# Packed attention and gated feed-forward in one kernel: another order of the first batch's small steps

## The chip, the cores and the metric

The kernel runs on one core of one Trainium2 chip. A core has TensorE (PE, matrix products; its weight loads are listed as PEld), VectorE (DVE), ScalarE (ACT), GpSimd (POOL) and SyncE (SP), which here issues nearly all DMAs. Each engine takes its own instructions in the order written, and waits on semaphores for the others. The metric is the device time of one launch in microseconds (us), the median of the runs shown.

## The reference

Eight batches, eight heads, 576 positions, head size 64. Every head packs its sequence into 32 rows and attends to these; the result goes through a gated feed-forward of width 1536.

```python
scale = 1.0 / np.sqrt(q.shape[-1])
def sm_attn(qq, kk, vv):
    s = scale * np.matmul(qq, kk.transpose(0, 1, 3, 2))
    s = s - np.max(s, axis=-1, keepdims=True)
    a = np.exp(s)
    a = a / (np.sum(a, axis=-1, keepdims=True) + 1e-09)
    return np.matmul(a, vv)
p_packed = sm_attn(p, k, v)                  # (8, 8, 32, 64)
out = sm_attn(q, p_packed, p_packed)         # (8, 8, 576, 64)
x = out.transpose(0, 2, 1, 3).reshape(4608, 512)
return ((x @ w_a) * (x @ w_b) @ w_out).astype(np.float32)
```

q, k, v and p arrive as float32. The three weight matrices arrive in 64 bits a number, and the kernel makes float32 of them itself.

## The kernel before

**Attention.** `stage1(b, e)` (L270 on) computes p_packed of batch `b` for one half `e` of the heads: scores on PE (L276), maximum on DVE (L282), exponential on ACT (L294), sums and reciprocal on DVE (L298, L301), transposes of the exponentials on PE (L315, L316), their copies to `a1T` by ACT (L317, L318), the product with v on PE (L325), and the scaling on DVE (L331). `turned` transposes p_packed (L262) and copies it to `ppT` (L264). `stage2(b, e)` is the second attention (L340 to L371). Both are Python generators: each `yield` ends a step, and the plan says when the next one is emitted.

**v.** The product at L325 reads tile `vt`, which `load_v` fills with four DMAs (two at L171 of 256 KB, two at L175 of 32 KB). From batch 1 on both halves share one buffer: half 1 of batch 1 can be loaded once the L325 of half 0 has read it.

**Weights.** They come in 36 pieces of 512 KB: four for each of the six chunks of two feature tiles (w_a and w_b), twelve for w_out. Step `A` (L203, ACT) and step `B` (L211 on ACT, or L208 on DVE or POOL, as the digit of `WAYS` for that piece says) prepare the two words, step `C` (L214, DVE) joins them to float32 in `w_ab` or `wo_f32`, and `D` (L239 on ACT, L91 on POOL) splits a piece of w_out into high and low parts. There are twelve piece buffers; each `C` frees one and asks for the next pieces (L224, L231).

**Feed-forward.** For batch 0, `g_tiles` (L395) multiplies ppT with a chunk of `w_ab`; `mm1` (L416) takes 24 products a feature tile, ACT and DVE make h from them (L428, L431, L435, L91), and `mm2_part` (L442) multiplies h with w_out: for each feature tile four token tiles with three products each, 12 products of 512 columns. All sums of one batch's feed-forward stand in PSUM until the last feature tile. The later batches use other forms of the same products (L766, L807).

**Order.** Nothing is scheduled by the framework: what Python emits is each engine's order. `START` is the list of steps before the first feature tile of batch 0. After that, `between()` is called twice for each feature tile in `mm1` (24 slots) and once for each of nine feature tiles in the second product, and emits the steps that `PLAN_0` has for this slot: `A` to `D`, the loads (`Lk`, `Lq`, `Lv`, `Lp`), `r0` and `r1` (next step of `stage1` of batch 1, half 0 or 1), `s0` and `s1` (the same for `stage2`), `k` and `q` (turns of k and q), `P0` (`turned`). Where a step stands in the list is where its instructions stand on every engine that it uses, DMA issues included. SP issues DMAs in that order; a buffer that isn't free holds up SP and all that stands behind.

Of the kernel before, what the change touches and what calls it, by code (L numbers as in the profile page):

```python
# [19 lines left out]
def tile_packed_attn_gated_ffn(  # L20
# [21 lines left out]
    B, H, S, D = q.shape  # L42
# [13 lines left out]
    NB = 2  # L56
# [36 lines left out]
    def bank():  # L93
        return ps_x.tile([P, 512], F32, name="x")

    def bank_pair(s=False):
        return ps_s.tile([P, 2, 512], F32, name="s") if s else ps_m.tile([P, 2, 512], F32, name="m")

    def work(b, name, shape, tag=None):
        if b == 0:  # L100
            return scratch.tile(shape, F32, name=name)
        return wk.tile(shape, F32, name=tag, bufs=2 if tag == "t1" else 1)
# [91 lines left out]
    def xT_cols(b, key, u, h, cols=slice(0, HS)):  # L194
        return xTs[b, key][h // R][64 * u:64 * u + 64, h % R, cols]
# [9 lines left out]
    def low_word(raw, way):  # L205
        low = raw[..., 0]
        if way:
            (nc.vector if way == 1 else nc.gpsimd).tensor_scalar(  # L208
                out=low, in0=low, scalar1=2.0 ** -29, scalar2=7.0, op0=ALU.mult, op1=ALU.min)
        else:  # L210
            nc.scalar.activation(out=low, in_=low, func=AF.Copy, scale=0.93 * 2.0 ** -29)  # L211
# [56 lines left out]
    def stage1(b, e):  # L268


        s = bank_pair(b or e == 0)
        first = b < 2
        parts = [(0, 0, 0, HS)] + ([(1, TR, 0, 2 * P), (1, 0, 2 * P, TR)] if first else [(1, 0, 0, HS)])
        for u, c, t, n in parts:
            for r in range(R):
                nc.tensor.matmul(  # L276
                    out=s[J * r:J * r + J, u, c:c + n], lhsT=pT[64 * u:64 * u + 64, 2 * r + e, :],
                    rhs=xT_cols(b, "k", u, 2 * r + e, slice(t, t + n)), start=True, stop=True)
        s = s[:, :, 0:HS]
        yield  # L280
        nmx = sm.tile([P, 1], F32, name="nmx")
        nc.vector.tensor_reduce(out=nmx, in_=s, axis=AXY, op=ALU.max)  # L282
        nc.vector.tensor_scalar(out=nmx, in0=nmx, scalar1=-scale, scalar2=None, op0=ALU.mult)
        if b > NB:
            yield
        a1 = work(b, f"a1_{e}", [P, S], "t1")
        rs = sm.tile([P, 1], F32, name="rs")
        if first:
            exps = [(a1, s, rs)]
        else:  # L290
            rs2 = sm.tile([P, 1], F32, name="rs2")
            exps = [(a1[:, 2 * TR:S], s[:, :, 0:2 * P], rs), (a1[:, 0:2 * TR], s[:, :, 2 * P:HS], rs2)]
        for dst, src, acc in exps:
            nc.scalar.activation(  # L294
                out=dst.rearrange("p (u t) -> p u t", u=2), in_=src, func=AF.Exp, bias=nmx, scale=scale, accum_out=acc)
        yield
        if first:
            nc.vector.tensor_scalar(out=rs, in0=rs, scalar1=1e-9, scalar2=None, op0=ALU.add)  # L298
        else:
            nc.vector.tensor_scalar(out=rs, in0=rs, scalar1=rs2, scalar2=1e-9, op0=ALU.add, op1=ALU.add)  # L300
        nc.vector.reciprocal(out=rs, in_=rs)  # L301
        yield
        a1T = work(b, f"a1T_{e}", [P, NT, P], "t2")
        rest = 2 * P if first else 0
        chunks = [P * i + ((HS + TR) * u if first else 2 * TR + 2 * P * u) for i in range(2) for u in range(2)]
        if b or e:
            pair = bank_pair(b)
            tp, tq = pair[:, 0, :], pair[:, 1, :]
        else:
            tp, tq = bank(), bank()  # L310
        if b == 0:
            chunks = [(HS + TR) * u + i for i in range(2) for u in range(2)]
        step = 1 if b else 2
        for i, c in enumerate(chunks):
            nc.tensor.transpose(tp[:, P * i:P * i + P], a1[:, c:c + step * (P - 1) + 1:step], ident)  # L315
        nc.tensor.transpose(tq[0:64, 0:P], a1[:, rest:rest + 2 * TR], ident)  # L316
        nc.scalar.copy(out=a1T[:, 0:4, :].rearrange("p i t -> p (i t)"), in_=tp)  # L317
        nc.scalar.copy(out=a1T[0:64, 4, :], in_=tq[0:64, 0:P])  # L318
        yield
        pps = bank_pair(True)[:, 0, :] if b else bank()  # L320
        vt = vts.pop((b, e))
        for i in range(NT):
            n = P if i < 4 else 64
            for r in range(R):
                nc.tensor.matmul(  # L325
                    out=pps[J * r:J * r + J, 0:D], lhsT=a1T[0:n, i, J * r:J * r + J],
                    rhs=vt[0:n, r, i, :], start=(i == 0), stop=(i == NT - 1))
        if e == 0:
            pp[b] = sm.tile([P, E + 1, D], F32, name="pp", bufs=1)
        for i in range(e, E + 1, E):  # L330
            nc.vector.tensor_scalar(out=pp[b][:, i, :], in0=pps[:, 0:D], scalar1=rs, scalar2=None, op0=ALU.mult)  # L331
        yield
# [145 lines left out]
    def drain(g):  # L478
        for _ in g:
            pass  # L480

    def emit(b, plan, tasks={}):

        for name in plan.split():
            if name in tasks:
                next(tasks[name], None)
                continue
            if name == "Z":
                warm_first()
                continue  # L490
            if name in "Ww":
                warm(9 if name == "W" else 1)
                continue
            if name in "ABCD":
                convert(name)
                continue
            what, e = name[:-1], int(name[-1])
            n = b + (e // 2 if b or what[0] == "L" else 0)
            if n >= B:
                continue  # L500
            if what == "S":
                if e == 0:
                    st[b] = [stage1(b, 0), stage1(b, 1), stage2(b, 0), stage2(b, 1)]
                next(st[b][e])
            elif what == "s":
                next(st[b][2 + e], None)
            elif what == "r":
                next(st[b][e], None)
            elif what == "T":
                turn_p(n)  # L510
            elif what == "P":
                turned(ppT[:, b % 2:b % 2 + 2], pp.pop(b), b % 2)
            elif what in ("k", "q"):
                turn(what, n, e % 2) if b else turn_first(what, e)
            elif what == "Lk":
                load(k, "k", n, e % 2)
            elif what == "Lq":
                load(q, "q", n, e % 2)
            elif what == "Lv":
                load_v(n, e % 2)  # L520
            elif what == "Lp":
                load_p(n)
# [8 lines left out]
        nc.tensor.matmul(out=x[:, 0:2 * P], lhsT=zero[:, 0:P], rhs=zero, start=True, stop=True)  # L531

    FIRST = ("k0 P0 K1 k2 q0 q1 v0 q2 v1 w1 w1 w1 w1 w1 w1 w1 w1 w1 w1 w1")
    START = ("Z Z Z Z T0 k0 k1 k2 k4 k3 q0 S0 S1 r0 r1 q1 q2 r1 r0 r0 r1 q4 r0 r1 q3 P0 s0 s1 B W A s0 B A A B s0 A s0 C B s1 C s1 s0 B C s1 A s1 B C Lp2 A A B s0 g s1 s0 g w s1 g C B B B C A Lk2 A C A B C A A B B Lk3 C C")
    WAYS = ("000000021020002100012012011200010010")
    TURN = ("1101110010")
    SUBS = ("0000")

    PLAN = (" |  |  | S0 | r0 | r0 |  | r0 |  | r0 Lv1 ; S1 | r1 | r1 q0 Lk2 | r1 | r1 | q1 Lk3 Lv2 P0 |  ; s0 | s0 s0 | s0 T2 | "
            "s0 Lp4 | s0 s1 | s1 s1 | s1 | s1 | s1 | t0 t1 t2 t3 u0 | k2 |  | k3 Lq2")  # L540
    PLAN = dict(enumerate(PLAN.split("|")))
    PLAN_0 = ("A | C C | B A B A | B C C B C | A A | C | B Lv0 | C B A T0 k0 Lp2 | A A B C Lq0 | C k1 | A B A B A C | S0 B | B A r0 | C C C | B A | | C C B r0 r0 D A A | S1 C D | B C B B A D | r1 C | A A D | r0 Lv1 Lq1 T2 | | q0 B r1 C B D r1 C | | A D B | C A r1 A B D | Lk2 B C B q1 D Lk3 A A P0 | C s0 s0 D C Lp4 A B | s1 s0 | Lv2 | D | s0 s1 s0 | k2 s0 s1 C k3 | s1 | | Lq2 D s0 s1 s1 Lq3 s1")
    PLAN_0 = dict(enumerate(PLAN_0.split("|")))

    pieces = [(c, n) for c in range(NC) for n in range(4)] + [(NC, f) for f in range(NFT)]
# [12 lines left out]
    def convert(x):  # L558
# [14 lines left out]
        elif x == "B":  # L573
            low_word(raw, int(WAYS[pieces.index((c, n))]))
        else:
# [18 lines left out]
    def next_g(b):  # L594

        if b:
            g_tiles(b, (0, 1), (2,), s=True)
            yield
            return
        late = []  # L600
        g_tiles(b, (0, 1), late=late)
        yield
        for x in late:
            lo_part(*x)
            yield
# [15 lines left out]
    tasks = {"g": next_g(0)}  # L621
    emit(0, START, tasks)
    drain(tasks["g"])
# [55 lines left out]
    for b in range(NB):  # L679
        plan = dict(PLAN if b else PLAN_0)  # L680
        slot, tasks, late_steps = [0], {"g": next_g(b + 1)} if b == 0 else {}, [""]
# [260 lines left out]
    for n in range(LAST):  # L942
        b, ft = NB + n // NFT, n % NFT
# [55 lines left out]
```

## Time and profile before

| | |
|---|---|
| median of 3 runs | 705.21 us (704.41 to 705.64) |
| profiled execution, whole | 705.02 us |
| its span on the core | 703.2 us |
| PE busy | 695.9 us (99%) |
| DVE, ACT, POOL busy | 448.5, 363.7, 412.7 us |
| HBM | 85.92 MB read, 15.73 MB written |

All times below count from the start of the span; 1.8 us of the execution lie outside it. An engine's busy time is the time in which an instruction of it runs; what stands in brackets behind an idle time is what ended it. The first batch's first product (L416) runs from 27.65 to 78.1 us, its second (L442) from 78.54 on; the sixteen DMA engines are busy nearly all of the time until then.

### The profile page before, as it was taken

How to read it: one execution, taken by the hardware profiler on the slowest of the kernel's cores; microseconds unless marked ns; L12 is line 12 of the kernel's file. 1: busy time of each engine (PE TensorE's matmuls, PEld its weight loads, DVE VectorE, ACT ScalarE, POOL GpSimd, SP SyncE). 2: the span in 40 equal slices, each digit the busy share in tenths (PEclk: the TensorE clock that was granted, in tenths of full speed). 3: DMA queues.
4: the chain of work that ended last, by engine and by line, in shares of the span. 5: the costliest groups of instructions: out<-in, count | busy, mean ns of one | idle time of the engine just before them, and what ended most of it. 6: DMA issues, size and time to landing. Idle time of an engine off the chain costs nothing.

```text
span 703.2 us, 14176 instructions
## 1 busy us (share of the span) xinstructions
PE 695.9 (99%) x5542; PEld 573.2 (82%) x5542; DVE 448.5 (64%) x822; ACT 363.7 (52%) x731; POOL 412.7 (59%) x323
## 2 busy tenths in 40 slices
PE   8999999999999999999999999999999999999998
PEld 6488878888788878888888887888888878888886
DVE  3998664567266679566765778665785667754432
ACT  4988734544244556545554455554545446544520
POOL 0557652337155778646864588655776578856520
PEclk9999999999999999999999999999999999999999
DMA  9999955677164727356434653556245323133002
GB/s 309 381 229 312 273 108 105 238 185 202 56 167 142 178 83 169 111 147 177 105 95 124 174 161 95 140 171 158 69 131 143 106 91 120 61 122 118 1 1 75
DMA packets 180371, 102.57 MB, mean 146 GB/s; under 512 B 145744, under 2 KB 161744, under 8 KB 174928
## 3 DMA queue, kind: packets, MB, share of 16 engines
q1 hardware_dynamic: 179888, 101.08, 50.7%
q8 instruction: 43, 0.70, 0.4%
q10 hardware_dynamic: 416, 0.59, 0.2%
q14 instruction: 24, 0.20, 0.1%
HBM read 85.92 MB, written 15.73 MB: 145 GB/s over the span
## 4 chain that ended last, share of the span: by engine, by line
PE 94%; ACT 1%; DVE 1%; POOL 1%; DMA 1%; issue 1%; SPq 0%; DVEq 0%; POOLq 0%; ACTq 0%
PE x L766 38%; PE m L807 30%; PE m L416 7%; PE x L821 5%; PE m L442 5%; PE s L325 2%; PE s L340 1%; PE m L592 1%; PE s L276 1%; PE x L395 1%; DMA raw<-in_moe_w_b_dram 1%; PE s L315 1%; POOL h_lo L91 1%; PE m L531 1%; DVE w_ab L214 0%
## 5 line engine op out<-in xcount | busy, mean ns | idle before, releaser
L766 PE MATMUL x<-wo,h_hi 128*128 128x512 f32 (+1 forms) x776 | 249.1, 391 | 0.0
L91 POOL TENSOR_TENSOR h_lo<-asb,h_hi 128x576 fp32r<-128x576 f32 x96 | 140.2, 1460 | 88.0 <-ACT h_hi L435 44.3
L766 PEld LDWEIGHTS x<-wo,h_hi 128*128 128x128 f32 x776 | 140.7, 188 | 21.8 <-ACT gs L827 0.9
L766 PE MATMUL x<-wo,h_lo 128*128 128x512 f32 (+1 forms) x388 | 152.1, 392 | 0.0
L91 POOL TENSOR_TENSOR G_lo<-gs,G_hi 128x640 fp32r<-128x640 f32 x72 | 112.8, 1572 | 30.7 <-ACT G_hi L842 30.4
L766 PEld LDWEIGHTS x<-wo,h_lo 128*128 128x128 f32 x388 | 72.9, 188 | 11.8
L91 POOL TENSOR_TENSOR A_lo<-gs,A_hi 128x256 fp32r<-128x256 f32 x36 | 27.1, 754 | 87.1 <-ACT A_hi L830 87.1
L889 DVE TENSOR_TENSOR d<-m,d 128x576 f32<-128x576 f32 (+1 forms) x73 | 54.1, 741 | 35.2 <-ACT d L885 34.5
L902 DVE TENSOR_TENSOR asb<-m,d 128x288 f32<-128x288 f32 x72 | 32.5, 451 | 65.4 <-ACT c L898 62.0
L898 ACT COPY c<-m 128x288 f32<-128x288 f32 x72 | 28.7, 399 | 82.5 <-PE m L807 82.5
L776 DVE TENSOR_TENSOR part<-x,part 128x512 f32<-128x512 f32 (+1 forms) x65 | 44.1, 678 | 38.5 <-PE x L766 38.5
L807 PE MATMUL m<-tx_hi,G_hi 128*128 128x288 f32 x216 | 63.8, 295 | 0.0
L807 PE MATMUL m<-tx_hi,G_lo 128*128 128x288 f32 x216 | 63.7, 295 | 0.0
L827 ACT COPY gs<-x 128x512 f32<-128x512 f32 x36 | 21.1, 587 | 81.6 <-PE x L821 81.6
L807 PE MATMUL m<-tx_lo,G_hi 128*128 128x288 f32 x216 | 63.3, 293 | 0.0
L842 ACT CAST G_hi<-gs 128x640 fp32r<-128x640 f32 x72 | 52.2, 729 | 15.0 <-POOL gs L836 14.5
L885 ACT COPY d<-m 128x576 f32<-128x576 f32 (+1 forms) x73 | 46.7, 639 | 20.0 <-PE m L807 19.7
L852 ACT CAST h_hi<-asb 128x576 fp32r<-128x576 f32 x72 | 49.0, 680 | 11.5 <-DVE asb L916 11.5
L807 PEld LDWEIGHTS m<-a_hi,G_hi 128*128 128x128 f32 x144 | 27.0, 187 | 31.8 <-issue 17.4
L836 POOL TENSOR_TENSOR gs<-gs 128x512 f32<-128x512 f32 x36 | 46.6, 1294 | 2.1 <-DVE gs L833 1.7
L807 PE MATMUL m<-a_hi,G_hi 128*128 128x288 f32 x144 | 46.6, 324 | 0.0
L915 DVE TENSOR_TENSOR m<-m,c 128x288 f32<-128x288 f32 x72 | 33.4, 464 | 16.4 <-PE m L807 14.7
(169 smaller groups left out, 1550.0 us busy)
## 6 DMA issues: line engine op xcount, KB each, us to landing
wr<-w_kept SPq DMA_DIRECT2D x36, 1024.0 KB, 5.1
nat<-in_k_dram SPq DMA_DIRECT2D x56, 144.0 KB, 5.0
nat<-in_q_dram SPq DMA_DIRECT2D x56, 144.0 KB, 5.3
vt<-in_v_dram SPq DMA_DIRECT2D x28, 256.0 KB, 3.6
out_dram<-part SPq DMA_DIRECT2D x27, 256.0 KB, 2.0
raw<-in_moe_w_a_dram SPq DMA_DIRECT2D x12, 512.0 KB, 7.7
raw<-in_moe_w_b_dram SPq DMA_DIRECT2D x12, 512.0 KB, 8.5
raw<-in_moe_w_out_dram SPq DMA_DIRECT2D x12, 512.0 KB, 7.2
```

The costliest lines, as they stand in the source:

```text
L91: return eng.tensor_tensor(out=dst, in0=src, in1=hi.bitcast(F32), op=ALU.subtract)
L416: nc.tensor.matmul(out=ps[:, half, 0:HS], lhsT=gt[:, kt, ft % 4, cols], rhs=at[:, kt, HS * half:HS * half + HS], start=(n == 0 and kt == 0 ...
L442: nc.tensor.matmul(out=o[:, cols], lhsT=ht[:, c0:c0 + P], rhs=wt[:, cols], start=(ft == 0 and n == 0), stop=(ft == NFT - 1 and n == 2))
L766: nc.tensor.matmul(out=o[:, cols], lhsT=ht[:, c0:c0 + P], rhs=wt[:, cols], start=(ft == fts[0] and n == 0), stop=end)
L776: nc.vector.tensor_tensor(out=parts[i][:, cols], in0=o[:, cols], in1=parts[i][:, cols], op=ALU.add)
L807: nc.tensor.matmul(out=bank[:, n % 2, 0:HS], lhsT=g, rhs=t, start=(first and i == 0), stop=(i == 2), skip_group_check=True)
L821: nc.tensor.matmul(out=gps[e][J * r:J * r + J, :], lhsT=ppT[rows, 2 * (b % 2), r, :], rhs=w[rows, r, :], start=True, stop=True)
L836: nc.gpsimd.tensor_tensor(out=gs[:, 2:4].rearrange("p a u f -> p a (u f)"), in0=gs[:, 0:2].rearrange("p a u f -> p a (u f)"), in1=s2.unsqu ...
L842: nc.scalar.copy(out=G_hi[:, n % 3], in_=gs[:, 1:6, n % 2])
L852: nc.scalar.copy(out=view(h_hi[ft]), in_=src)
L885: nc.scalar.copy(out=d[:, both], in_=X[:, both, 0:HS])
L889: nc.vector.tensor_tensor(out=d[:, both], in0=V[:, both, 0:HS], in1=d[:, both], op=ALU.add)
```

## The change

Only lists of numbers and letters change, and one `yield`. The exponential of batch 1's half 0 becomes a step of its own; the last part of START has fewer conversions and PLAN_0's first slots have more; two pieces take another way in step `B`; and in PLAN_0 the steps of `stage1` of batch 1 stand in other slots.

```diff
         nc.vector.tensor_scalar(out=nmx, in0=nmx, scalar1=-scale, scalar2=None, op0=ALU.mult)
-        if b > NB:
+        if b > NB or (b, e) == (1, 0):
             yield
...
-    START = ("Z Z Z Z T0 k0 k1 k2 k4 k3 q0 S0 S1 r0 r1 q1 q2 r1 r0 r0 r1 q4 r0 r1 q3 P0 s0 s1 B W A s0 B A A B s0 A s0 C B s1 C s1 s0 B C s1 A s1 B C Lp2 A A B s0 g s1 s0 g w s1 g C B B B C A Lk2 A C A B C A A B B Lk3 C C")
-    WAYS = ("000000021020002100012012011200010010")
+    START = ("Z Z Z Z T0 k0 k1 k2 k4 k3 q0 S0 S1 r0 r1 q1 q2 r1 r0 r0 r1 q4 r0 r1 q3 P0 s0 s1 B W A s0 B A A B s0 A s0 C B s1 C s1 s0 B C s1 A s1 B C Lp2 A A B s0 g s1 s0 g w s1 g C B C A Lk2 A C A C B B A B Lk3")
+    WAYS = ("000000021000202100010012011200010010")
...
-    PLAN_0 = ("A | C C | B A B A | B C C B C | A A | C | B Lv0 | C B A T0 k0 Lp2 | A A B C Lq0 | C k1 | A B A B A C | S0 B | B A r0 | C C C | B A | | C C B r0 r0 D A A | S1 C D | B C B B A D | r1 C | A A D | r0 Lv1 Lq1 T2 | | q0 B r1 C B D r1 C | | A D B | C A r1 A B D | Lk2 B C B q1 D Lk3 A A P0 | C s0 s0 D C Lp4 A B | s1 s0 | Lv2 | D | s0 s1 s0 | k2 s0 s1 C k3 | s1 | | Lq2 D s0 s1 s1 Lq3 s1")
+    PLAN_0 = ("A B B | C C C | A B A B A | C B C C B | A A | C C | B Lv0 | C B A T0 k0 Lp2 | A A B C Lq0 | C | C | k1 A | A B | S0 C r0 A | r0 B A B B | C C | C r0 r0 B A | S1 C B A | D A B A B | r1 C | D A B | r0 Lv1 Lq1 T2 | C D A | q0 B r1 C B D r1 C | D r1 C | A D B | C A A B D | Lk2 P0 B C B q1 D Lk3 A A | C s0 s0 D C Lp4 A B | s1 s0 | Lv2 | D | s0 s1 s0 | k2 s0 s1 C k3 | s1 | | Lq2 D s0 s1 s1 Lq3 s1")
```

The first place is DVE at the start of batch 0's first product. The pieces of the second chunk are raw_139 (its join stands just ahead of these rows in both programs), raw_141, raw_143 and raw_145; raw_147 to raw_151 belong to the third. Before:

```order
L208 TENSOR_SCALAR raw_147<-raw_147 128x512
L214 SCALAR_TENSOR_TENSOR w_ab_95<-raw_141 128x2x256
L214 SCALAR_TENSOR_TENSOR w_ab_95<-raw_143 128x2x256
L214 SCALAR_TENSOR_TENSOR w_ab_95<-raw_145 128x2x256
L214 SCALAR_TENSOR_TENSOR w_ab_95<-raw_147 128x2x256
L214 SCALAR_TENSOR_TENSOR w_ab_95<-raw_149 128x2x256
L431 TENSOR_TENSOR asb_512<-m_520,asb_512 128x576
```

And with the change:

```order
L214 SCALAR_TENSOR_TENSOR w_ab_95<-raw_141 128x2x256
L214 SCALAR_TENSOR_TENSOR w_ab_95<-raw_143 128x2x256
L214 SCALAR_TENSOR_TENSOR w_ab_95<-raw_145 128x2x256
L208 TENSOR_SCALAR raw_147<-raw_147 128x512
L431 TENSOR_TENSOR asb_503<-m_511,asb_503 128x576
L214 SCALAR_TENSOR_TENSOR w_ab_95<-raw_147 128x2x256
L214 SCALAR_TENSOR_TENSOR w_ab_95<-raw_149 128x2x256
```

The word step of a third-chunk piece moves from ahead of three joins of the second chunk to behind them, and two joins of the third chunk move behind the first product's DVE step.

The second place is PE at the start of the second product of batch 0, whose rows are L442 (h_hi0, h_hi1, ... are the feature tiles); L316 and L325 belong to half 1 of batch 1's `stage1`, and L262 to its `turned`. Before:

```order
L316 MATMUL s_1166<-ident_90,t1_1047 64x128
L442 MATMUL m_1176<-wo_951,h_hi0_488 128x512 x2
...
L442 MATMUL m_1176<-wo_987,h_hi1_490 128x512 x2
...
L442 MATMUL m_1177<-wo_1025,h_lo2_493 128x512
L325 MATMUL s_1222<-vt_1112,t2_1165 32x64 x20
L442 MATMUL m_1176<-wo_1069,h_hi3_494 128x512 x2
...
L442 MATMUL m_1177<-wo_1069,h_lo3_495 128x512
L262 MATMUL x_1282<-ident_90,pp_1109 128x128 x2
```

With the change:

```order
L316 MATMUL s_1161<-ident_90,t1_1036 64x128
L442 MATMUL m_1171<-wo_1010,h_hi0_479 128x512 x2
...
L442 MATMUL m_1172<-wo_1010,h_lo0_480 128x512
L325 MATMUL s_1188<-vt_1101,t2_1160 32x64 x20
L442 MATMUL m_1171<-wo_1056,h_hi1_481 128x512 x2
...
L442 MATMUL m_1172<-wo_1157,h_lo3_486 128x512
L262 MATMUL x_1266<-ident_90,pp_1098 128x128 x2
```

The product with v stood behind three feature tiles (36 products) and stands behind one (12); the transposes at L262 stay behind four.

The third place is SP at the loads of the last pieces of w_out and of v for half 1 of batch 1, as a difference of the two programs:

```order
-L231 DMA raw_870<-in_moe_w_out_dram 128x1024
-L231 DMA raw_935<-in_moe_w_out_dram 128x1024
-L171 DMA vt_1112<-in_v_dram 128x4x128 x2
-L175 DMA vt_1112<-in_v_dram 32x4x64 x2
-L116 DMA nat1_1117<-in_q_dram 32x36x32 x4
+L231 DMA raw_915<-in_moe_w_out_dram 128x1024
+L231 DMA raw_933<-in_moe_w_out_dram 128x1024
+L171 DMA vt_1101<-in_v_dram 128x4x128 x2
+L175 DMA vt_1101<-in_v_dram 32x4x64 x2
+L116 DMA nat1_1106<-in_q_dram 32x36x32 x4
```

Only the numbers of the buffers differ: SP's order of loads is the same through the whole program.

## Rows read from the trace of the kernel before

**Rows 1.** Page: busy time of the engines, and the granted clock by slices.
```profile
PE 695.9 (99%) x5542; PEld 573.2 (82%) x5542; DVE 448.5 (64%) x822; ACT 363.7 (52%) x731; POOL 412.7 (59%) x323
...
PEclk9999999999999999999999999999999999999999
```
**Rows 2.** Waits of PE: in total, times, longest (us).
```profile
PE x L395 <- DVE w_ab L214: 1.2, 1, 1.2
```
**Rows 3.** Timeline of PE, 31 to 42 us: start, duration, line.
```profile
31.06 0.42 PE L416 MATMUL m<-a_hi,glo 128*128 128x288 f32 x2
32.65 1.66 PE L395 MATMUL x<-w_ab,ppT 64*32 64x512 f32 x16 [1.17 <-DVE w_ab L214]
...
40.82 1.09 PE L395 MATMUL x<-w_ab,ppT 64*32 64x512 f32 x16
```
**Rows 4.** Timeline of DVE, 29 to 35 us.
```profile
29.97 1.09 DVE L214 SCALAR_TENSOR_TENSOR w_ab<-raw 128x512 uint32<-128x512 uint32 x1
30.98 0.42 DVE L208 TENSOR_SCALAR raw<-raw 128x512 uint32<-128x512 uint32 x1
31.32 3.17 DVE L214 SCALAR_TENSOR_TENSOR w_ab<-raw 128x512 uint32<-128x512 uint32 x5
```
**Rows 5.** Timeline of PE, 78 to 88 us.
```profile
78.54 0.70 PE L442 MATMUL m<-wo,h_hi 128*128 128x512 f32 x2
...
86.91 0.90 PE L325 MATMUL s<-vt,t 128*32 128x64 f32 x40
87.74 0.73 PE L442 MATMUL m<-wo,h_hi 128*128 128x512 f32 x2
```
**Rows 6.** Timeline of SP's DMA issues, 70 to 90 us.
```profile
71.27 3.34 SPq L231 DMA_DIRECT2D raw<-in_moe_w_out_dram  x6
74.90 0.97 SPq L171 DMA_DIRECT2D vt<-in_v_dram  x2
```
**Rows 7.** Instructions of tile vt, issued 74.5 to 90 us: durations (ns), first and last start.
```profile
L171 SPq DMA_DIRECT2D vt<-in_v_dram x2: 378/458/538, 74.9 to 75.3; - x2
L175 SPq DMA_DIRECT2D vt<-in_v_dram x2: 439/1844/3249, 76.0 to 79.3; - x2
...
DMA to landing us min/median/max: 6.1/9.3/9.7
```
**Rows 8.** Stretches: busy time of each engine, granted clock, DMA share, GB/s.
```profile
75.00:80.00 5.00, 5.00 (x35) 4.72 (x35) 3.59 (x7) 3.18 (x6) 2.79 (x3) 1.00 1.01 406
80.00:85.00 5.00, 5.00 (x23) 4.13 (x22) 2.85 (x6) 3.07 (x7) 2.62 (x2) 1.00 1.01 276
```
**Rows 9.** Timeline of ACT, 80 to 84 us.
```profile
81.96 0.62 ACT L239 CAST wo<-wo_f 128x512 fp32r<-128x512 f32 x1 [1.02 <-DVE wo_f L214]
82.49 0.58 ACT L317 COPY t<-s 128x512 f32<-128x512 f32 x1
82.97 0.26 ACT L318 COPY t<-s 64x128 f32<-64x128 f32 x1
```
**Rows 10.** Stretches at the end: PE's busy time first, clock third from the end.
```profile
700.00:701.00 1.00, 0.01 (x1) 0.00 (x0) 0.42 (x1) 0.00 (x0) 0.00 (x0) 1.00 0.35 112
...
702.00:703.00 1.00, 0.00 (x0) 0.00 (x0) 0.00 (x0) 0.00 (x0) 0.00 (x0) 0.73 0.00 0
703.00:704.00 1.00, 0.00 (x0) 0.00 (x0) 0.00 (x0) 0.00 (x0) 0.00 (x0) 0.50 0.00 0
```
**Rows 11.** Timeline of PE in the first 26 us.
```profile
1.19 3.78 PE L531 MATMUL m<-zero 128*128 128x256 f32 x8 [1.19 <-DVE zero L609]
...
5.19 1.50 PE L153 MATMUL x<-ident,kn 128*128 128x128 f32 x8
6.53 0.60 PE L153 MATMUL m<-ident,kn 128*128 128x128 f32 x4
6.96 0.39 PE L153 MATMUL x<-ident,kn 128*128 128x128 f32 x2
...
17.91 7.99 PE L592 MATMUL m<-kn,ident 128*128 128x512 f32 x18
```

## The prediction, made before the changed kernel ran

> **What bounds the kernel now.** I read the page first, then PE's waits, then PE's timeline over batch 0, and last the queue that feeds it. PE is busy 695.9 of 703.2 us, at the full clock in every slice [rows 1], so a change can give back only what PE idles, and costs whatever it makes PE wait, one for one: after batch 0 nothing has slack to catch up with. The longest idle stretch that these lists touch stands at 31.5 us: L395 of the second chunk waits 1.17 us for a join in `w_ab` [rows 2, 3], and then takes 1.66 us where the next one takes 1.09 [rows 3], since its second half waits again for the last join. That is 1.17 + 0.57 = 1.74 us to win, and no more; from there to the end of batch 0's second product PE's timeline runs without a gap worth naming. Beside PE stands the DMA queue: it is full (share 1.01) in the stretches around 80 us [rows 8], and what is issued there lands 6 to 10 us later [rows 7].
>
> **The change part by part.**
>
> *The second chunk's joins first.* Before, DVE runs one join of the chunk (29.97, 1.09 us), a word step of 0.42 us (it holds up the row behind it by 0.34, from 30.98 to 31.32), and then five joins in 3.17 us, 0.63 each, of which the second and the third are what PE waits for [rows 4]. The word step goes behind: 0.34 us less. The first join's 1.09 us are 0.46 more than its neighbours take; if that excess goes too, the gain is 0.80, otherwise 0.34. I take 0.7, nearer to the common row of 0.63. Fewer conversions in START and more in the first slots shift ACT and DVE work by one feature tile; ACT's and DVE's totals stay, and PE's products cover them as they do now; price nothing, and if the cover fails, the idle of rows 3 again (at most 1.7).
>
> *The yield.* It only lets the exponential of batch 1's half 0 stand apart from its maximum. No instruction is added. Price nothing: half 0 has slots to spare ahead of its L325.
>
> *Batch 1's half 1, one slot group earlier.* This is the part that decides. L325 of half 1 needs two things: the copies of the exponentials by ACT and v. Before, PE comes to it after 36 products, at 86.91 [rows 5]. These 36 take 86.91 - 78.54 = 8.37 us, 0.2325 each [rows 5]. With the change it comes after 12: 78.54 - 0.7 + 12 x 0.2325 = 80.6 us.
>
> What is v doing at 80.6? Its four DMAs stand behind six pieces of w_out on SP (3.34 us of issues from 71.27) and are issued at 74.9, 75.3, 76.0 and 79.3 [rows 6, 7]. They land 6.1 to 9.7 us after their issue [rows 7], the last one issued with the least: 74.9 + 9.3 = 84.2 for the first, 79.3 + 6.1 = 85.4 for the last. SP's order is the same in both programs. Can the load come sooner because half 0's L325 frees the buffer sooner? SP is busy with w_out until 71.27 + 3.34 = 74.6, so by 0.3 us in issue at most; and as the transfers ahead keep the queue full [rows 8], by less in landing. The edit can't speed up these transfers: no byte ahead of them goes away. So the DMA sets PE's time here, whatever is won at 31 us:
>
> - PE idles from 80.6 to 84.2, does a part of L325, and waits for the rest until 85.4.
> - L325 takes 87.74 - 86.91 = 0.83 us in five steps [rows 5]; the last, 0.2, runs behind the last landing: 85.6.
> - Of the 36 products that before stood ahead of L325, 24 are now behind it: 24 x 0.2325 = 5.6 us, done at 91.2.
> - Before, PE was there at 87.74 [rows 5]. So it is 91.2 - 87.74 = 3.4 us later, and the 0.7 us won early are swallowed by the wait.
>
> Profiled execution 705.02 + 3.4 = 708.4; it stands 0.2 under the median of the runs, so 708.6 beside that.
>
> *The clock.* An idle of 3.6 us, followed by 1.4 us in which PE does 0.8 us of work in pieces, may lower PE's clock. [...] The 1.17 us of rows 3 left it at full [rows 1]. At the start, PE runs 8 rows of 256 columns in 3.78 us, 0.47 each, while a row of 512 columns takes 7.99 / 18 = 0.44 later: half speed. The eight transposes from 5.19 take 1.34 us to the next row, 0.17 each, the four from 6.53 take 0.11 each [rows 11]: full speed from about 6.1, after 4.9 us of work at half. If the clock falls at 80 to 85 and returns in the same manner, PE loses half of 4.9, 2.4 us. The ends are 0 (it stays) and 2.4; above 1.00 it can't go. The idle is longer than that of rows 10, so I take the fall, and 2.1 for it, near the start's row. Sum: 708.6 + 2.1 = 710.7 us.
>
> [...]
>
> *Scaling and ppT copy ahead of joins and q's turn.* In the rows behind L325, the DVE steps L331 and L264 move ahead of one w_out join or q's turn. L262 stays behind the fourth feature tile, and 24 products now separate it from L325 more than before, so nothing waits for these steps; price nothing.
>
> **Rivals.**
>
> *The clock stays up.* The stall is the same, its price 3.4: 708.6 us. For it: the pieces of L325 that run at 84.2 and 85.0. Against it: rows 10.
>
> *ACT's copies are the wait, not v.* If v did land in time, L325 would still need L317 and L318, which end at 82.97 + 0.26 = 83.2 before, behind a split of w_out that waits 1.02 us for a join [rows 9]; the change leaves these rows in that order. Then L325 ends at 83.2 + 0.8 = 84.0, and 84.0 + 5.6 - 87.74 = 1.9 us: 707.1. Against it: v's 85.4.
>
> *Faster.* The earlier joins free piece buffers earlier, w_out and then v come some 5 us earlier, ACT's copies with them, and PE keeps what it won at 31 us: 0.8 to 1.74 us, 704.4 to 703.5. It decides from the point at which v has landed by 80.6. Against it: the transfers, not the buffers, fill the queue; rows 8 show no gap that could be closed.
>
> *No change.* The wait moves PE only by what it won: it needs v at about 82.7 and the copies too; 705.
>
> *Worse.* The clock falls, returns late or twice, and batch 1's second attention, now behind a late L325, holds up the next product as well: over 712.4.
>
> **How the numbers follow.** Forecast 0.64 (710.7); clock stays 0.17 (708.6); ACT's copies 0.05 (707.1); faster 0.05; no change 0.03; worse 0.06. What a measurement of this kernel can tell from no change is about 0.2%, 1.4 us. Range 706.9 to 712.4: it holds the first three cases; the forecast alone spans 709.6 to 711.4. Slower 0.92, same 0.03, faster 0.05.
>
> **What would show it.** In PE's timeline of the changed kernel, L395 at about 32 us should be idle ahead by under 0.6 us instead of 1.17, and batch 0's second product begin before 78.2. Then an idle stretch of 3 us or more ahead of L325, ended by vt's DMA near 84 us, with smaller ones inside it; behind it L442 rows of about 0.43 us each for some microseconds, with a granted clock under 1.00 in that slice of the page. vt's issues should stand at about 75 us as now. Wrong would be: v landed before PE gets to L325 (then faster); the idle put down to ACT L317 (then 1.9); or a clock of 1.00 throughout (then 3.4).

## The result, and the profile after

The changed kernel takes 710.93 us (median of 5 runs, 710.78 to 712.65) against 705.21 of the kernel before in the same runs (704.41 to 705.84): a ratio of 1.0088, with a 95% interval of 1.0073 to 1.0103. It is slower by 5.7 us, and the forecast of 710.7 is 0.2 off. The profiled execution has a span of 709.0 us instead of 703.2, 5.8 more.

The page of the changed kernel, busy time by engine, answers to [rows 1]:

```profile
PE 698.2 (98%) x5542; PEld 575.0 (81%) x5542; DVE 448.7 (63%) x822; ACT 364.3 (51%) x732; POOL 410.5 (58%) x322
```

The work is the same, but for one step in all that moved from GpSimd to ScalarE (three digits of `WAYS` differ, not two: two steps `B` go to ScalarE and one to GpSimd). PE is busy for 2.3 us more, and the rest of the 5.8 us must be idle time. PE's waits say which (total, times, longest), beside [rows 2]:

```profile
PE s L325 <- DMA vt<-in_v_dram: 4.1, 1, 4.1
...
PE m L416 <- ACT asb L428: 0.6, 2, 0.4
...
PE x L395 <- DVE w_ab L214: 0.4, 1, 0.4
```

A wait of 4.1 us for v is new, and the wait of 1.2 us for the joins is down to 0.4. PE's timeline of the changed kernel, at the places of [rows 3] and [rows 5]:

```profile
31.88 1.67 PE L395 MATMUL x<-w_ab,ppT 64*32 64x512 f32 x16 [0.44 <-DVE w_ab L214]
...
78.37 0.70 PE L442 MATMUL m<-wo,h_hi 128*128 128x512 f32 x2
...
81.17 0.39 PE L442 MATMUL m<-wo,h_lo 128*128 128x512 f32 x1
85.69 1.69 PE L325 MATMUL s<-vt,t 128*32 128x64 f32 x40 [4.13 <-DMA vt<-in_v_dram]
87.31 1.22 PE L442 MATMUL m<-wo,h_hi 128*128 128x512 f32 x2
88.33 0.63 PE L442 MATMUL m<-wo,h_lo 128*128 128x512 f32 x1
...
90.93 0.62 PE L442 MATMUL m<-wo,h_hi 128*128 128x512 f32 x2
...
93.65 0.62 PE L442 MATMUL m<-wo,h_hi 128*128 128x512 f32 x2
```

PE is through with 12 products at 81.56 and starts L325 at 85.69. L325 takes 1.62 us to the next row instead of 0.83, and the first row of two products 1.22 instead of 0.73. At 93.65 PE has 36 products and L325 behind it; before, that was at 87.74 [rows 5]. The difference, 5.9 us, is the whole loss: behind it almost nothing is lost or won (5.8 at the end of the span).

The granted clock shows why these rows are long. Stretches of 1 us of the changed kernel (length, busy time of PE, PEld, DVE, ACT and POOL, granted clock, DMA share, GB/s):

```profile
84.00:85.00 1.00, 0.00 (x0) 0.00 (x0) 0.51 (x1) 0.00 (x0) 0.46 (x1) 1.00 1.17 126
85.00:86.00 1.00, 0.31 (x13) 0.34 (x16) 0.18 (x1) 0.79 (x2) 0.09 (x1) 0.81 0.15 31
86.00:87.00 1.00, 0.99 (x35) 0.58 (x28) 0.00 (x0) 0.41 (x1) 1.00 (x1) 0.50 0.93 147
87.00:88.00 1.00, 1.00 (x12) 0.73 (x11) 0.56 (x2) 0.00 (x0) 0.19 (x1) 0.50 0.92 148
88.00:89.00 1.00, 1.00 (x4) 0.81 (x3) 0.67 (x2) 0.64 (x2) 0.00 (x0) 0.50 0.92 146
89.00:90.00 1.00, 1.00 (x5) 0.83 (x5) 0.00 (x0) 1.00 (x3) 0.94 (x1) 0.99 1.03 164
```

The granted clock falls within the microsecond in which PE begins to work again, from 1.00 to 0.50, and is back at 89 (0.99). The page's row of granted clock by slices still shows only nines: a fall of 3.4 us inside a slice of 17.7 us (a mean of 0.90) isn't seen there. The profile is of the shortest of the five runs (710.78, a mean granted clock of 0.998 over the span). Of the other four, one has 0.998 too, and three have 0.995, 0.995 and 0.994 (710.93, 711.45 and 712.65): by an estimate from these means, they spent 7 to 9 us at a clock of 0.50. Where, and behind what wait, wasn't profiled.

Tile vt of the changed kernel, at the place of [rows 7]:

```profile
L171 SPq DMA_DIRECT2D vt<-in_v_dram x2: 429/493/557, 75.4 to 75.9; - x2
L175 SPq DMA_DIRECT2D vt<-in_v_dram x2: 432/2108/3784, 76.5 to 80.3; - x2
...
DMA to landing us min/median/max: 6.4/10.1/10.5
```

v is issued at 75.4, 0.5 later than before. Its first DMA by itself takes 10.2 us, so v lands first at 75.4 + 10.2 = 85.6, and last at 80.3 + 6.4 = 86.7.

### The profile page after: what moved, and what is told of

Same layout as the page of the kernel before. It is cut to its first block, busy times and chain, and to the rows that moved or that the text cites. A ratio compares the mean times of both kernels' runs of the same rounds, so it can differ in the third digit from the quotient of the medians.

```text
span 709.0 us, 14171 instructions
## 1 busy us (share of the span) xinstructions
PE 698.2 (98%) x5542; PEld 575.0 (81%) x5542; DVE 448.7 (63%) x822; ACT 364.3 (51%) x732; POOL 410.5 (58%) x322
## 4 chain that ended last, share of the span: by engine, by line
PE 90%; DMA 7%; ACT 1%; SPq 0%; issue 0%; DVE 0%; DVEq 0%; ACTq 0%
PE x L766 37%; PE m L807 29%; PE m L416 8%; PE x L821 5%; PE m L442 4%; DMA raw<-in_moe_w_a_dram 4%; DMA vt<-in_v_dram 3%; PE s L325 2%; PE s L340 1%; PE s L276 1%; PE x L395 1%; PE s L315 1%; DMA raw<-in_moe_w_b_dram 1%; ACT raw L203 0%; SPq L140 0%
## 5 line engine op out<-in xcount | busy, mean ns | idle before, releaser
L91 POOL TENSOR_TENSOR h_lo<-asb,h_hi 128x576 fp32r<-128x576 f32 x96 | 140.9, 1467 | 88.8 <-ACT h_hi L852 43.3
L91 POOL TENSOR_TENSOR G_lo<-gs,G_hi 128x640 fp32r<-128x640 f32 x72 | 112.8, 1573 | 30.7 <-ACT G_hi L842 30.4
L91 POOL TENSOR_TENSOR A_lo<-gs,A_hi 128x256 fp32r<-128x256 f32 x36 | 27.2, 755 | 86.9 <-ACT A_hi L830 86.7
L416 PE MATMUL m<-a_hi,ghi 128*128 128x288 f32 x192 | 43.1, 306 | 0.7 <-ACT asb L428 0.6
```

What stands on the lines that cost most here:

```text
L91: return eng.tensor_tensor(out=dst, in0=src, in1=hi.bitcast(F32), op=ALU.subtract)
L416: nc.tensor.matmul(out=ps[:, half, 0:HS], lhsT=gt[:, kt, ft % 4, cols], rhs=at[:, kt, HS * half:HS * half + HS], start=(n == 0 and kt == 0 ...
```

## The experiments

The theory: the whole loss comes from one step, the product with v two slots earlier, which waits for a load that stands behind w_out. Its rivals: the new order of the joins is itself at fault; v is only one of two waits there, with ScalarE's copies behind it; and the clock's share is all or none of it. Slots are counted from 0; the diffs show the slots of `PLAN_0` around the edit. The medians:

| run | us | against before, 95% interval |
|---|---|---|
| e1_late | 705.66 | 1.0007 (0.9998 to 1.0015) |
| e2_two | 706.73 | 1.0022 (1.0010 to 1.0034) |
| e3_before_early | 711.53 | 1.0082 (1.0068 to 1.0096) |
| e4_filled | 709.28 | 1.0053 (1.0041 to 1.0065) |
| e5_v_ahead | 707.61 | 1.0032 (1.0020 to 1.0044) |
| e6_v_copies | 705.58 | 1.0003 (0.9994 to 1.0011) |
| e7_turn_first | 705.00 | 0.9995 (0.9987 to 1.0004) |
| e8_two_v_copies | 705.46 | 1.0003 (0.9995 to 1.0012) |
| e9_turn_ahead | 704.59 | 0.9993 (0.9984 to 1.0002) |
| e10_two_ahead | 704.67 | 0.9993 (0.9984 to 1.0002) |

**One step put back, one step alone.** e1_late, the changed kernel with the product in its old slot:

```diff
 slots 24 to 26
-| D r1 C | A D B | C A A B D |
+| D C | A D B | C A r1 A B D |
```

> The changed kernel with one step put back: the product of half 1 of batch 1 with v (L325) two slots later, after 36 products of w_out as before; the new order of the joins, the new steps of batch 0 and the yield stay. Theory (the early product that waits for v is the whole loss): the wait of 4.1 us and the fall of the clock go, and what is left is the 0.17 us by which the products with w_out begin earlier, up to the 0.77 at the first product with w_ab: 704.4 to 705.3 us, no stretch at half clock between 80 and 95 us. Rival (the new order of the joins and of batch 0's steps is itself slower, and v's landing 1.3 us later comes from it): v's wait stays 1 us or more also at the later place, 706.5 to 710.

e3_before_early, the kernel before with that step alone:

```diff
 slots 24 to 26
-| | A D B | C A r1 A B D |
+| r1 | A D B | C A A B D |
```

> The kernel before with one step moved: the product with v of batch 1's half 1 two slots earlier, after 12 products of w_out instead of 36; nothing else of the change. Theory: the wait of 3.4 to 4.2 us and the half clock come with this step alone: 709.5 to 711.5 us, with a stretch at half clock behind the wait. Rival (the loss needs the new order of the joins, through the DMA queue that then brings v later): 705 to 707.

Measured: 705.66 and 711.53 (709.99 to 713.34), the latter at the upper end of its range. The step alone brings the loss, and without it the loss is gone. The new order of the joins is not at fault. The profile of e3_before_early is of its longest run, 713.34. Its rows of PE and of tile vt show the same wait and the same landing behind it:

```profile
86.80 1.68 PE L325 MATMUL s<-vt,t 128*32 128x64 f32 x40 [3.81 <-ACT wo L239]
88.42 1.22 PE L442 MATMUL m<-wo,h_hi 128*128 128x512 f32 x2
...
93.44 0.63 PE L442 MATMUL m<-wo,h_hi 128*128 128x512 f32 x2
```

```profile
L171 SPq DMA_DIRECT2D vt<-in_v_dram x2: 492/512/532, 76.9 to 77.5; - x2
...
DMA to landing us min/median/max: 6.4/9.7/10.0
```

Here a name in brackets is to be doubted. The wait is put down to a split of w_out (L239), which ended at 86.75 by chance; L325 doesn't read it. What it needs of ScalarE, L318, was done at 84.7, and v's first DMA, taken with the median of 9.7 us, lands at about 76.9 + 9.7 = 86.6. It is v again.

e1_late was expected at 704.4 to 705.3 and is 0.4 above. PE begins w_out's products 1.3 us earlier than before in it (77.25 instead of 78.54), and loses this again; e7 to e10 show where.

**The place between.** e2_two puts the product behind 24 products:

```diff
 slots 24 and 25
-| D r1 C | A D B |
+| D C | A D r1 B |
```

> The changed kernel with the product with v one slot later, after 24 products of w_out instead of 12. Theory: TensorE reaches it at about 81.6 + 12 x 0.23 = 84.3 us and v lands at about 86.7 at the latest, so it waits 1.3 to 1.5 us (4.1 in the changed kernel), and the clock falls for less or not at all: 706.0 to 707.5 us. Rival (the price of the place is the same wherever it stands before w_out's other products): 710 to 711. Rival (only the clock counts, and it stays here): 705 to 706.

Measured: 706.73, runs from 705.7 to 709.6. In the profiled run, one of the shorter ones (706.1), v's landings leave two waits, of 0.56 us (until 84.48) and 0.22, and the clock stays at 1.00. So the price is the distance to v's landing, not the place. The runs spread over 4 us. The three longest (708.37 to 709.60) have a mean granted clock of 0.998 over the span, the others 0.999 or 1.000, so the clock fell for a time in those three; how long PE waited in them wasn't profiled.

**The clock by itself.** e4_filled lays 18 further products, whose results are discarded, behind the 12 and directly ahead of L325 (its expectation has them ahead of the 12; the rows below show 80.39, behind them):

```diff
+            if name == "V":
+                x = bank()
+                for _ in range(18):
+                    nc.tensor.matmul(out=x, lhsT=h_hi[0][:, 64:64 + P], rhs=wo_hi[0], start=True, stop=True)
+                continue
...
 slot 24
-| D r1 C |
+| V D r1 C |
```

> The changed kernel with 18 further products of 128 columns by 512, whose results are discarded, ahead of the 12 products of w_out that stand before the product with v: some 4.2 us of TensorE work laid into the wait. The kernel's own work is unchanged. Theory: the wait falls under 0.5 us, its time is filled and not saved, and the clock does not fall: the time falls by the clock's share alone. If that is the 2.1 us of the prediction: 708.6 to 709.0; if it is the 1.2 us that is left of the loss once the wait's share is taken off: 709.5 to 709.9. Rival (the clock costs nothing here): 710.9 or more.

Measured: 709.28, between the theory's two ranges and in neither, 1.65 under the changed kernel (1.5 between the spans of the profiled runs, 707.5 and 709.0), with a granted clock of 1.00 throughout. PE of e4_filled, to be held against the rows of the changed kernel above (L494 are the further products):

```profile
80.39 4.24 PE L494 MATMUL x<-wo,h_hi 128*128 128x512 f32 x18
84.56 0.43 PE L325 MATMUL s<-vt,t 128*32 128x64 f32 x16
85.76 0.82 PE L325 MATMUL s<-vt,t 128*32 128x64 f32 x24 [0.77 <-DMA vt<-in_v_dram]
86.51 0.73 PE L442 MATMUL m<-wo,h_hi 128*128 128x512 f32 x2
...
89.37 0.61 PE L442 MATMUL m<-wo,h_hi 128*128 128x512 f32 x2
```

From the end of L325 the first 12 products take 89.37 - 86.51 = 2.86 us here and 90.93 - 87.31 = 3.62 in the changed kernel: 0.76 for the clock. L325 is done 0.80 earlier here, but v also landed earlier:

```profile
L175 SPq DMA_DIRECT2D vt<-in_v_dram x2: 431/1823/3215, 75.6 to 78.8; - x2
...
DMA to landing us min/median/max: 7.3/10.2/11.0
```

78.8 + 7.3 = 86.1 instead of 86.7. How much of the 0.80 is v's, the weight loads (PEld) of the second part of L325 show, which wait for v's second DMA in both runs. The changed kernel first, then e4_filled:

```profile
86.35 0.42 PEld L325 LDWEIGHTS s<-vt,t 128*32 128x32 f32 x16 [0.25 <-DMA vt<-in_v_dram]
...
85.76 0.27 PEld L325 LDWEIGHTS s<-vt,t 128*32 128x32 f32 x16 [0.93 <-DMA vt<-in_v_dram]
```

v releases them 0.59 later in the changed kernel, and 0.2 of the 0.80 are left for the clock. So the clock cost 0.76 + 0.2 = 1.0 us in the profiled run of the changed kernel, and 0.6 of the 1.5 between the two spans is v's landing. In e3_before_early the same sum gives more: 12 products in 93.44 - 88.42 = 5.02 instead of 2.86, 2.2 us, and again 0.2 in L325 (taken from the changed kernel, since L325 takes 1.62 us to the next row in both): 2.4 us. Its clock came back only at 93 (0.50 until then, 0.94 in 93 to 94).

**v in time.** The other way to take the wait away leaves the product early and brings v earlier. Two new letters hold back the weight loads that the slots in between ask for, until v's four DMAs are issued. e5_v_ahead:

```diff
+    held = []
...
     def load_pieces(n):
+        if held:
+            held[0] += n
+            return
...
+            if name == "H":
+                held.append(0)
+                continue
+            if name == "G":
+                load_pieces(held.pop())
+                continue
...
 slot 13, slot 21
-| S0 C r0 A |
+| H S0 C r0 A |
...
-| r0 Lv1 Lq1 T2 |
+| r0 Lv1 G Lq1 T2 |
```

> The changed kernel with only the order of SP's loads altered: the last four of the six w_out pieces in front of the load of v's half 1 are issued behind it; the product with v keeps its early place. Four pieces land 1.27 us apart, so v lands about 5 us earlier (81.6 instead of 86.7 at the latest), if the w_out pieces that now come later are not missed by the joins. Theory (v's landing behind w_out is the wait): TensorE no longer waits for v, but for ScalarE's copies of the transposed block (L317 and L318, which end at 83.8 in the changed kernel), some 2.2 us instead of 4.1, with no or less half clock behind it: 707.0 to 709.1 us. Rival (the place of the product costs what it costs, whatever v does): 710 to 711.5. Rival (v was all, the copies are in time): 704.5 to 705.5.

Measured: 707.61 (706.3 to 709.1). Tile vt, PE and ACT of e5_v_ahead, and its stretches, with the columns as above:

```profile
L171 SPq DMA_DIRECT2D vt<-in_v_dram x2: 379/439/499, 74.2 to 74.6; - x2
L175 SPq DMA_DIRECT2D vt<-in_v_dram x2: 430/462/495, 75.2 to 75.7; - x2
...
DMA to landing us min/median/max: 3.8/4.1/4.5
```

```profile
83.26 0.90 PE L325 MATMUL s<-vt,t 128*32 128x64 f32 x40 [2.26 <-ACT t L318]
...
89.66 0.62 PE L442 MATMUL m<-wo,h_hi 128*128 128x512 f32 x2
```

```profile
81.95 0.62 ACT L239 CAST wo<-wo_f 128x512 fp32r<-128x512 f32 x1 [1.09 <-DVE wo_f L214]
82.47 0.58 ACT L317 COPY t<-s 128x512 f32<-128x512 f32 x1
82.95 0.26 ACT L318 COPY t<-s 64x128 f32<-64x128 f32 x1
```

```profile
80.00:85.00 5.00, 2.74 (x49) 1.92 (x48) 2.80 (x4) 2.44 (x6) 2.64 (x2) 1.00 1.02 330
85.00:90.00 5.00, 5.00 (x24) 4.13 (x23) 1.58 (x3) 3.16 (x6) 2.59 (x2) 1.00 0.71 118
```

v has landed by about 79.5, and now PE waits 2.26 us for L318, as the prediction's rival had it, with the clock up. That is the profiled run, 706.80, one of the shorter ones. The four longer ones (707.56 to 709.08) have a mean granted clock of 0.997 or 0.998, so in them the clock fell for a time, and the median holds a share of that. A second wait stood behind the first. e6_v_copies takes it away too, by the order of ScalarE:

```diff
 slot 23, on top of e5_v_ahead
-| q0 B r1 C B D r1 C |
+| q0 B r1 C r1 B D C |
```

> As the run with v's load ahead of four w_out pieces, and on ScalarE the two copies of the transposed block (L317 and L318) ahead of the last w_out split (L239) and one low-word step (L211); nothing else. Theory: the copies end at about 82.0 instead of 83.8, both things the product needs are there within 0.9 us of its turn, no half clock: 705.0 to 706.3 us. Rival (the copies don't matter): the same as the run before, within 0.5 us.

Measured: 705.58. L318 ends at 80.4 and L325 starts at 80.46 without a wait. So with both operands in time the early place costs nothing that these runs show (interval 0.9994 to 1.0011), and gains nothing either.

**Where the early gain goes.** In e1_late, e6_v_copies and e8_two_v_copies PE waits later on for the turn of q's second half (L124), which VectorE does behind a w_out join. DVE of e1_late:

```profile
88.90 0.69 DVE L214 SCALAR_TENSOR_TENSOR wo_f<-raw 128x512 uint32<-128x512 uint32 x1 [1.72 <-POOL wo L91]
89.51 0.28 DVE L331 TENSOR_SCALAR pp<-s,rs 128x64 f32<-128x64 f32 x1
90.32 0.42 DVE L264 COPY ppT<-x 128x256 f32<-128x256 f32 x1 [0.53 <-PE x L262]
91.65 0.69 DVE L214 SCALAR_TENSOR_TENSOR wo_f<-raw 128x512 uint32<-128x512 uint32 x1 [0.91 <-POOL wo L91]
92.26 0.42 DVE L208 TENSOR_SCALAR raw<-raw 128x512 uint32<-128x512 uint32 x1
92.60 1.37 DVE L124 STREAM_TRANSPOSE xT<-nat 128x1152 f32<-128x1152 f32 x1
```

The join waits for GpSimd (0.91) and the turn waits behind it, with an idle engine. The edits, on e1_late for e7 and e9, on e6_v_copies for e8, and on e8_two_v_copies for e10:

```diff
 slot 27, e7_turn_first
-| Lk2 P0 B C B q1 D Lk3 A A |
+| Lk2 P0 q1 B C B D Lk3 A A |
...
 slots 24 and 25, e8_two_v_copies
-| D r1 C | A D B |
+| D C | A D r1 B |
...
 slot 27, e9_turn_ahead and e10_two_ahead
-| Lk2 P0 B C B q1 D Lk3 A A |
+| Lk2 q1 P0 B C B D Lk3 A A |
```

> The changed kernel with the product with v in its late place, as in the run named e1_late, and on VectorE the turn of q's second half (L124) ahead of a w_out join (L214) and a low-word step (L208). In e1_late TensorE begins the products with w_out 1.3 us earlier than before the change and is 0.3 us later behind q's products (L340), since L124 starts at 92.6 there and at 90.4 before. Theory (the turn behind the join is what takes the early gain back): L124 starts at about 90.7, L340 does not wait, 0.6 to 1.0 us off e1_late: 704.5 to 705.1 us, under the kernel before by 0.3 to 1.0. Rival (the gain is lost to the loads anyway, or to the join that is now behind the turn): 705.4 to 706.0.

> v's load ahead of four w_out pieces and the two copies earlier on ScalarE, and the product with v after 24 products of w_out (12 in the changed kernel, 36 before). Theory: nothing is waited for at the product, and the DVE steps behind it keep their early place, so the early gain at the first product with w_ab (0.8 to 1.1 us) is kept: 704.2 to 705.0 us, below the kernel before. Rival (the w_out pieces that come later, or the DMA queue, take it back): 705.3 to 706.5.

> The changed kernel with the product with v in its late place, and on VectorE the turn of q's second half (L124) between the scaling of batch 1's sums (L331) and the copy of ppT (L264), where VectorE stands idle; e7_turn_first has it behind the copy, and the w_out join behind it starts 0.65 us later than in e1_late. Theory (the chain of w_out's joins is the next limit: join on VectorE, split on ScalarE, low part on GpSimd, 2.75 us a piece, so the delay of that join comes out at the last piece at 107 us): the join starts at about 91.7 us, the last low part ends early enough, no gap at 107, and 0.3 us come off e7_turn_first: 704.4 to 704.9. Rival (the 0.3 us are lost elsewhere): 704.9 to 705.4, the same as e7_turn_first.

> The kernel of e8_two_v_copies (v's load ahead of four w_out pieces, the two copies earlier on ScalarE, the product with v after 24 products) with the turn of q's second half ahead of the copy of ppT. In e8_two_v_copies TensorE waits 0.77 us for that turn. Theory: that wait goes and nothing takes its place, 0.6 to 0.8 us off: 704.6 to 704.9 us. Rival (q lands too late, since its load is behind the w_out pieces, or the copy of ppT is then late): 705.2 to 705.6.

Measured: 705.00 for e7, in its theory's range; 705.46 for e8, a miss of its theory (704.2 to 705.0) and in its rival's range, though for another reason than the rival's: L340 waits 0.77 us for the turn there, which I hadn't seen coming; 704.59 for e9 and 704.67 for e10, in the ranges of their theories. e10 is 0.8 under e8. e9 is 0.4 under e7, but the runs of both spread over more than 1 us (704.31 to 706.20 and 704.34 to 705.51), so that e9's place of the turn beats e7's isn't shown by the times. In e7 the join behind the turn starts at 92.30, and PE's row of two products at 107.25 takes 0.92 instead of 0.62, while the last low part of w_out ends at 107.6. In e10 a smaller one of 0.21 has its name in the trace. PE of e10_two_ahead, and POOL:

```profile
107.31 0.50 PE L442 MATMUL m<-wo,h_hi 128*128 128x512 f32 x1 [0.21 <-POOL wo L91]
```

```profile
103.22 1.29 POOL L91 TENSOR_TENSOR wo<-wo_f,wo 128x512 fp32r<-128x512 f32 x1
105.96 1.29 POOL L91 TENSOR_TENSOR wo<-wo_f,wo 128x512 fp32r<-128x512 f32 x1 [1.46 <-ACT wo L239]
```

The pieces come 2.75 us apart (join, split, low part, in one buffer), and PE uses one in 12 x 0.2325 = 2.79 us. So the early gain meets a chain that is hardly faster than PE. e9 and e10 are the best versions: 0.6 to 0.7 us under the kernel before by their medians, but both intervals hold 1, so it is not shown that they beat it. Against the changed kernel they win 6.3 us.

## Why the prediction was right

**The joins.** 0.7 us taken; L395 of the second chunk starts 32.65 - 31.88 = 0.77 earlier. The excess of the first join is gone, and with it the GpSimd word step that ran beside it (see the last section). DVE of the changed kernel, beside [rows 4]:

```profile
29.94 2.48 DVE L214 SCALAR_TENSOR_TENSOR w_ab<-raw 128x512 uint32<-128x512 uint32 x4
32.35 0.52 DVE L208 TENSOR_SCALAR raw<-raw 128x512 uint32<-128x512 uint32 x1
```

Four joins in 2.41 us. But the "timeline without a gap" from there to the second product didn't hold: PE waits 0.6 us for ACT's L428 in the first product (0.2 to 0.8 in the experiments), and of the 0.77 only 0.17 are left at 78.37, so the sign "before 78.2" didn't come. The sum needed none of it, since the wait for v swallows it.

**The wait for v.** The mechanism, the place and the releaser are as predicted. The size was 3.4 and is larger: PE is 5.9 us late at 93.65, and 1.0 of this is the clock's, so 4.9 are the wait's. Of the 1.5 that the term lacked, 1.3 are v's landing. I took 84.2 to 85.4 from the kernel before, and it was 85.6 to 86.7, though the issues were only 0.5 to 1.0 later. The load's time from issue to landing differed with what stood ahead of it (6.4 to 10.5 us here, at a DMA share of 1.03 and 1.11 in 75 to 80 and 80 to 85; 3.8 to 4.5 in e5_v_ahead behind four pieces fewer), and isn't a constant that can be moved to another run. In e1_late and e4_filled v's first landing, by issue and median time, was at about 74.3 + 9.9 = 84.2 and 74.3 + 10.2 = 84.5, and in e2_two the wait for it ended at 84.48, so the landing also moves from run to run. The other 0.2 is that not only the last of L325's five steps stands behind a landing: the third already waits for v's second DMA, and three steps are left behind it.

**The clock.** 2.1 taken, between 0 and 2.4. No run shows the 2.1, which was my estimate: the clock fell, to 0.50 as at the end of [rows 10], but cost 1.0 us in the profiled run; in e3_before_early, whose profile is of its longest run, it cost 2.4, the upper bound. The bound's reason doesn't hold: I had the time of return from the slow rows at the start of the program [rows 11], but the granted clock of the kernel before is 1.00 in every stretch of 2 us from 0 to 20, so no row shows that those rows were slow by the clock, and the two runs return after 3.4 and 6.8 us at half clock instead of 4.9. So one term was 1.5 too small and the other 1.1 too large, and that 710.7 came so near is in part luck. Behind the wait of 4.13 us the granted clock was 0.50, and behind the one of 3.81 in e3_before_early too. Behind the one of 2.26 in the profiled run of e5_v_ahead it stayed at 1.00, and so it did at the end of the changed kernel, from 705.8, where PE's work is over, to 709.0. So from the fall of [rows 10] alone, the one at 85.7 couldn't be told.

**The rivals.** ACT's copies as the wait were priced at 1.9 us, 707.1, and given 0.05 because v is later. e5_v_ahead, where v is in time, has this wait, and PE's place of 87.74 comes at 89.66 in it, 1.9 late, in a run of 706.80. The faster case asked for v by 80.6 and for the copies with it; e6_v_copies has both and is no faster than before, so that rival's last step, PE keeps what it won, was wrong too.

**Scaling and ppT copy.** Priced at nothing, and in the changed kernel nothing waits for them. The cover was the stall itself. With the stall gone, VectorE's order in these rows is worth 0.7 to 0.9 us, each run held against the kernel before in its own runs: e1_late is 0.2 above it and e9_turn_ahead 0.7 under, e8_two_v_copies 0.1 above and e10_two_ahead 0.6 under.

## What to carry to other kernels

Before a consumer is moved ahead on TensorE, read when each of its operands lands, on which queue, and behind what; the issue time said little here, with landings 6.4 to 10.5 us behind it in one order of the loads and 3.8 to 4.5 in another. Behind the wait that the trace names there can be a second one that it hides (2.26 us behind the 4.13 here), so both have to go before the move can pay. Time that is won early in a program is kept only if every later chain that feeds TensorE has room for it (here 2.75 us a piece against TensorE's 2.79). And a profile is one run: before its terms are taken for the median's, hold its granted clock against that of the other runs.

## What the runs showed of the hardware

Joins on VectorE that started 0.06 to 0.11 us behind the start of a GpSimd L91 ran long: 1.90 us in the kernel before (at 73.63), 1.91 in the changed one (at 76.59) and 1.87 in e6_v_copies. DVE and POOL of e6_v_copies:

```profile
79.54 1.87 DVE L214 SCALAR_TENSOR_TENSOR wo_f<-raw 128x512 uint32<-128x512 uint32 x1
...
83.46 0.69 DVE L214 SCALAR_TENSOR_TENSOR wo_f<-raw 128x512 uint32<-128x512 uint32 x1 [2.06 <-POOL wo L91]
```

```profile
79.43 1.43 POOL L91 TENSOR_TENSOR h_lo<-asb,h_hi 128x576 fp32r<-128x576 f32 x1
```

The first join ends at 81.41, 0.55 behind the end of L91 at 80.86, and takes 1.87 instead of the 0.69 of the second, which starts behind the end of another L91 (82.14 + 1.29 = 83.43). Beside a GpSimd word step (L208) the excess was smaller. In the kernel before, joins that start 0.10, 0.22 and 0.31 us behind the start of such a step take 1.09, 0.99 and 0.94 us (at 29.97, 53.60 and 70.48) and end about 0.8 us ahead of its end; the first of them is the excess of [rows 4]. In the changed kernel no GpSimd instruction runs beside the four joins from 29.94 (the next L208 starts at 32.75), and they take 0.6 each. Why a join runs long beside these steps, and why it ends behind L91 but ahead of the word step, no run shows.

An issue took SP itself for longer where more stood ahead of it. The longer of L175's two issues takes 3.78 us in the changed kernel and 0.50 in e5_v_ahead, where four pieces of w_out fewer stand ahead of it on SP; the instruction and its bytes are the same.
